# TensorE's next work chosen by the state of banks and engines, products paced by due dates, gelu's 0.5 moved, v kept as two fp16 parts

## The chip, the cores and the metric

One core of a Trainium2 chip runs the whole program. The engines named here are TensorE (PE; its weight loads are PEld), VectorE (DVE), ScalarE (ACT), GpSimd (POOL) and SyncE (SP, which issues the DMAs). The metric is device time in microseconds (us): the median of three runs, lower is better.

## The reference

```python
x = A_x                                               # 1 x 2048 x 512
sa, ca, ga, sb, cb, gb = split(silu(c) @ w_mod, 6)
h = layernorm(x) * (1 + ca) + sa
q, k, v = heads(h @ A_wqkv)                            # 32 heads of 16
x = x + ga * (softmax(q @ k.T * 16 ** -0.5) @ v) @ A_wo
h = layernorm(x) * (1 + cb) + sb
g = shift(gelu(layernorm(h) @ B_w1))                   # quarters moved by +1, -1, +2, -2 rows
x1 = h + g @ B_w2
B = x1 + gelu(layernorm(x1) @ B_w3) @ B_w4             # 1792 hidden columns
out = x + gb * B
```

All of it is in float32, and gelu is the tanh form. Work that feeds TensorE is split into a high and a low part, so that each product of the layers takes three matmuls (high by high, high by low, low by high; the lines of `mm3`).

## The kernel before, in words

The 2048 rows of x are four chunks (`ci`) of 512 queries, the 32 heads are 16 pairs (`pr`), and a chunk with a pair is a unit (`u`): 64 units in all. A unit takes 16 steps, one for each 128 keys; step `s` runs from 0 to 1023. Each step has two rows, one for each head of the pair (`j`), and a row is a pair of matmuls that run side by side on the two halves of the array: a score product `sc` of step `s` (line 1021, keys by queries), and a product `mb` of step `s + LEAD`, 24 steps ahead (line 1005), whose maximum over keys is taken only to know the softmax's shift before the scores come. So there are 2048 rows of `sc` and 2048 of `mb`, and the first 48 rows hold `mb` alone.

What the other engines do with a row: ACT takes the exponential of `sc` into `pt` (line 1017), DVE takes the maximum of `mb` into `mx` (line 1001). The result of the exponential is a 32-bit number whose upper 16 bits serve directly as an fp16 factor; the lower 16 bits are made into a second fp16 factor by `p_low` (line 1072) on POOL, or, when POOL is predicted to be over `LACT` = 800 ns behind ACT, in two halves on ACT (line 127, a helper's). Then TensorE multiplies by v: for each step a pass with the upper factor (line 1098), for each two steps a pass with the lower (line 1095), each pass being four matmuls that run side by side on four column strips of the array. They accumulate in `pv`, one bank for a unit; at its end ACT copies it out (`ac`, line 1116), TensorE transposes it (`ot`, line 1127), DVE sums the parts (`sm`, line 1134) and POOL scales them (line 1138).

PSUM has eight banks: one for `pv` and seven (`NSM`) that rows and all other products share (`Slots`); three rows need six.

All other products (k, q, v of later heads and chunks, the rows of the modulation, and for each finished chunk the tail: A_wo, layer norms, B_w1, B_w2, B_w3, B_w4) are generators in a list of the planner `Sched`. It runs while the kernel is built and writes out one fixed order for each engine; nothing is chosen on the chip. The planner keeps a time for each engine, prices each piece, and hands out the consumers' operations (`chain`, `misc`) to ACT, DVE and POOL when it believes them ready. On the chip each engine follows its list in order, and waits at an instruction until the semaphores are there.

The main loop before goes over fixed blocks of three rows (`GRP`). After each second block come the passes with v that are due (`LAG` blocks behind), and then `fill` adds other products as long as a credit lasts, which grows by a fixed amount for each step (`SC0`, `TAILB`). If the planner thinks that the banks of a block come late, `gap` adds other products ahead of it.

v is kept in DRAM as `Vs`, 192 columns of bf16 for a pair: three bf16 parts, 20 columns apart (`VD`), and an fp16 copy for the pass with the lower factor. `v_tiles` makes it: ACT writes the first part and the fp16 copy, DVE the remainder `vr`, ACT the second part (line 773), POOL the third (line 774).

Gelu's factor 0.5 is multiplied into w2 and w4 when these are prepared (`pieces_gen`, line 899).

Of the kernel before, what the change touches and what calls it, by code (L numbers as in the profile page):

```python
# [8 lines left out]
F32 = mybir.dt.float32  # L9
# [24 lines left out]
VHI = 2.0 ** 39  # L34
VMAX = 2.0 ** 14
VD = 20

SC0 = (32, 900.0, 700.0)
TAILB = (0.0, 500.0, 560.0, 590.0)
# [40 lines left out]
VP = 2  # L80
XB = 4


class Sched:
# [4 lines left out]
    def __init__(self):  # L89
        self.pend = []  # L90
        self.chains = []
        self.gens = []
        self.credit = 0.0
        self.T = {"P": 0.0, "A": 0.0, "D": 0.0, "G": 0.0, "S": 1000.0}
        self.end = 0.0
        self.banks(8)

# [86 lines left out]
    def one(self):  # L184

        self.marks()
        for g in list(self.gens):
# [11 lines left out]
            else:  # L199
                self.credit -= v  # L200
                self.T["P"] += v
# [109 lines left out]
def kernel(ctx, tc, A_x, A_wqkv, A_wo, B_w1, B_w2, B_w3, B_w4, c, w_mod, out):  # L311
# [48 lines left out]
    def v_lo(t):  # L360
        return t[:, :, 128:192].bitcast(F16).rearrange("p a (b n) -> p a b n", b=2)
# [19 lines left out]
    Vs = dr.tile([NP, P, NKT, 192], BF16, name="Vs")  # L381
# [94 lines left out]
    zero = con.tile([4, CH], F32, name="zero")  # L476
# [239 lines left out]
    for i in range(NV):  # L716
        t = qp.tile([P, H // 4, 192], BF16, name=f"vt{i}")
        pool.memset(t, 0.0)
        pool.memset(v_hi(t)[:, :, :, DH:DH + 1], VHI)
        pool.memset(v_lo(t)[:, :, :, 8 + DH:9 + DH], 1.0)  # L720
# [8 lines left out]
    vlive, vrs = [], [0]  # L729
    direct, near = [], set()  # L730

    def v_tiles(w, a, kts):
        wh, wl = halves(w, KT)
        for kt in kts:
            ci, t = divmod(kt, TPC)
            h = hT[ci]
            yield lambda: len(vlive) < NV and vrs[0] < 2 and sch.room() and ("hT", ci) in done
            vrs[0] += 1
# [9 lines left out]
            r = qp.tile([P, H // 4, 2, DH], F32, name="vr", tag="vr", bufs=2)  # L748

            def rest(v=v, b3=b3, r=r, b=b):  # L750
                dve.tensor_tensor(r, b3, v[:, :, :, 0:DH], op=OP.subtract)
                sch.free(b)

            def store(kt=kt, w=w):
                vrs[0] -= 1

# [4 lines left out]
                def gone():  # L761
                    vlive.remove(kt)
                    done.add(("vk", a, kt))
                    if kt % 4 == 3:
# [6 lines left out]
                      ("A", cA(256), lambda vl=vl, b3=b3: act.activation(vl[:, :, :, 8:8 + DH], b3, AF.Copy, scale=1.0 / VHI)),  # L771
                      ("D", cD(256), rest),
                      ("A", cA(256), lambda v=v, r=r: act.activation(v[:, :, :, VD:VD + DH], r, AF.Copy)),
                      ("G", cG(256), lambda v=v, r=r: pool.tensor_tensor(v[:, :, :, 2 * VD:2 * VD + DH], r, v[:, :, :, VD:VD + DH],
                                                                         op=OP.subtract)),
# [97 lines left out]
    def pieces_gen():  # L873
        while True:
# [23 lines left out]
            if nm in ("w2", "w4"):  # L898
                ops.append(("A", cA(), lambda f=f: act.activation(f, f, AF.Copy, scale=0.5)))
# [57 lines left out]
    vst = [at.tile([P, NKT // 4, 192], BF16, name=f"vst{i}") for i in range(4)]  # L957
# [745 lines left out]
```

## Time and profile before

| | us |
|---|---|
| median of three runs | 2002.66 (2001.76 to 2005.11) |
| span of the profiled execution, first to last instruction | 2000.7 |
| start, up to the first score product | 98.2 |
| from the first to the last score product | 1744.5 |
| after the last score product (tail of the last chunk) | 158.0 |
| mean granted TensorE clock | 0.986 of full speed |

The profile has no time of its own for the execution beside the span; the span is 2.0 us under the median. In the rows that follow, a busy time is the union of an engine's instructions. A matmul's end is modelled, and matmuls overlap, so that 96% for PE does not mean that the array is always fed: the distance from one matmul's start to the next one's says more. "Idle before" and the waits name what an engine stood idle for.

### The profile page before, as it was taken

To read this page: it belongs to the slowest core of one execution; us is meant where nothing else is said; L and a number is where in the kernel's file an instruction comes from. 1 tells how busy PE (TensorE), PEld (TensorE's weight loads), DVE (VectorE), ACT (ScalarE), POOL (GpSimd) and SP (SyncE) were. 2 spreads that over 40 slices of the span, in tenths; PEclk is the share of its full clock that TensorE was granted. 3 is DMA by queue.
4 is the path that set the end of the run, shared out by engine and by line. 5 is a ranking of instruction groups with operands and counts; after the bars stand their busy time and mean duration, and the time that the engine had idled before them with its cause. 6 is when DMAs were issued, how large, how long until landed. Compare 5 with 4: busy or idle time off the path is not lost.

```text
span 2000.7 us, 42354 instructions
## 1 busy us (share of the span) xinstructions
PE 1920.9 (96%) x14480; PEld 1146.7 (57%) x14480; DVE 1652.2 (83%) x3010; ACT 1473.6 (74%) x3083; POOL 1676.1 (84%) x1609
## 2 busy tenths in 40 slices
PE   7999999999999999999999999999999999999899
PEld 4655555555455555555455555555555555555798
DVE  7887988888899888888989898898898889883643
ACT  5376888777878777777878787786787878777443
POOL 6287999889999998888999998898899989888532
PEclk8999999999999999999999999999999999999999
DMA  5767677766643334345433333334433343334432
GB/s 184 205 201 228 182 231 218 244 225 192 198 157 111 115 103 143 109 136 162 126 111 92 109 111 114 115 119 148 157 98 100 115 151 107 121 95 147 149 146 90
DMA packets 232352, 293.24 MB, mean 147 GB/s; under 512 B 125876, under 2 KB 177076, under 8 KB 215848
## 3 DMA queue, kind: packets, MB, share of 16 engines
q1 hardware_dynamic: 232136, 290.53, 46.4%
q8 instruction: 115, 1.88, 0.4%
q14 instruction: 101, 0.83, 0.1%
HBM read 225.81 MB, written 62.91 MB: 144 GB/s over the span
## 4 chain that ended last, share of the span: by engine, by line
PE 67%; DVE 16%; ACT 8%; issue 3%; POOL 2%; DMA 2%; SPq 1%; POOLq 0%; ACTq 0%; DVEq 0%
PE mb L1005 14%; PE sc L1021 10%; PE pv L1098 10%; DVE mx L1001 9%; PE w L339 7%; PE w L343 6%; PE w L341 6%; PE pv L1095 4%; ACT pt L1017 4%; POOL pt L1072 2%; DVE xs L1421 1%; DVE sq L1418 1%; DMA vst<-Vs 1%; PE mr L644 1%; PE ot L1127 1%
## 5 line engine op out<-in xcount | busy, mean ns | idle before, releaser
L1072 POOL TENSOR_SCALAR pt<-pt 128x1024 f16<-128x1024 uint16 x988 | 1312.5, 1365 | 132.6 <-ACT pt L1017 125.4
L1001 DVE TENSOR_REDUCE mx<-mb 128x1 f32<-128x512 f32 x2048 | 1281.0, 683 | 76.0 <-PE mb L1005 54.5
L1017 ACT ACTIVATE pt<-sc 128x512 int32<-128x512 f32 x2048 | 1090.8, 606 | 272.3 <-PE mb L1005 164.9
L1005 PE MATMUL mb<-kst,qtl 64*128 64x512 f32 x2048 | 752.1, 454 | 49.0 <-ACT pt L1017 16.1
L1021 PE MATMUL sc<-qtl,kst 64*128 64x512 f32 x2048 | 716.4, 444 | 2.6 <-DVE A L329 0.6
L1005 PEld LDWEIGHTS mb<-kst,qtl 64*128 64x128 f32 x2048 | 348.7, 193 | 254.5 <-DVE mx L1001 91.4
L1021 PEld LDWEIGHTS sc<-qtl,kst 64*128 64x128 f32 x2048 | 335.6, 186 | 153.5 <-DVE mx L1001 47.1
L1098 PE MATMUL pv<-pt,vst 128*32 128x512 f16 x4096 | 358.2, 397 | 0.1
L1095 PE MATMUL pv<-pt,vst 128*17 128x512 f16 (+1 forms) x2048 | 213.7, 394 | 2.2 <-POOL pt L1072 1.7
L1098 PEld LDWEIGHTS <-vst 128*32 128x32 bf16 x4096 | 90.9, 95 | 167.6 <-issue 108.8
L339 PE MATMUL w<-A,wr 128*128 128x256 f32 (+2 forms) x576 | 175.3, 304 | 0.3 <-ACT A L333 0.3
L1428 POOL TENSOR_TENSOR g<-xs,g 128x256 fp32r<-128x256 f32 (+2 forms) x144 | 103.2, 718 | 83.4 <-ACT g L1427 81.3
L341 PE MATMUL w<-A,wr 128*128 128x256 f32 (+2 forms) x576 | 169.8, 295 | 0.5 <-DVE A L329 0.3
L343 PE MATMUL w<-A,wr 128*128 128x256 f32 (+2 forms) x576 | 167.7, 291 | 0.0
L339 PEld LDWEIGHTS w<-A,wr 128*128 128x128 f32 x576 | 109.6, 190 | 35.4 <-DVE mx L1001 10.3
L339 PE MATMUL w<-wr,g 128*128 128x512 f32 x288 | 119.2, 414 | 0.6 <-ACT g L1427 0.6
L341 PEld LDWEIGHTS w<-A,wr 128*128 128x128 f32 x576 | 109.9, 191 | 12.4 <-issue 11.3
L343 PE MATMUL w<-wr,g 128*128 128x512 f32 x288 | 114.7, 398 | 0.2 <-POOL g L1428 0.2
L341 PE MATMUL w<-wr,g 128*128 128x512 f32 x288 | 113.6, 394 | 0.0
L343 PEld LDWEIGHTS w<-A,wr 128*128 128x128 f32 x576 | 109.8, 191 | 6.7 <-issue 6.7
L1535 DVE TENSOR_TENSOR x<-x,w 128x512 f32<-128x512 f32 x64 | 43.9, 687 | 82.0 <-PE w L343 82.0
L1424 ACT ACTIVATE sq<-w 128x256 f32<-128x256 f32 (+2 forms) x144 | 55.7, 387 | 68.8 <-PE w L343 66.0
(151 smaller groups left out, 2103.8 us busy)
## 6 DMA issues: line engine op xcount, KB each, us to landing
wr<-Ws SPq DMA_DIRECT2D x80, 1024.0 KB
kst<-Ks SPq DMA_DIRECT2D x189, 256.0 KB
vst<-Vs SPq DMA_DIRECT2D x252, 192.0 KB
qtl<-Qs SPq DMA_DIRECT2D x192, 64.0 KB
Vs<-vt SPq DMA_DIRECT2D x32, 384.0 KB
Ws<-wq SPq DMA_DIRECT2D x40, 256.0 KB
Ws<-wst SPq DMA_DIRECT2D x40, 256.0 KB
wst<-in_B_w_dram SPq DMA_DIRECT2D x36, 256.0 KB
```

The lines of the kernel that those rows point to most:

```text
L339: te.matmul(o, lh, rh, start=first, stop=False)
L341: te.matmul(o, lh, rl, start=False, stop=False)
L343: te.matmul(o, ll, rh, start=False, stop=last)
L1001: end = sch.crit("D", 605, e + PX, lambda: dve.reduce_max(mxs[u][:, j, g, c:c + 1], b, axis=AX.X))
L1005: return ready, lambda: te.matmul(b, lhs, kst[u % 3][r, c * CH:(c + 1) * CH], start=True, stop=True), after
L1017: ea = sch.crit("A", 480, e + PX, lambda: act.activation(pt[s][:, j], b, AF.Exp))
L1021: return ready, lambda: te.matmul(b, kst[u % 3][r, kt * P:(kt + 1) * P], qst[u][r], start=True, stop=True), after
L1072: e_low[s] = XP["G"] + sch.crit("G", 1345, ready, lambda: pool.tensor_scalar(o, i, 0.5, 1.0, op0=OP.mult, op1=OP.mult))
L1095: te.matmul(acc[r:r + n, :], v[:, (kt + i) % 4, c - n:c].bitcast(F16), pt[s + i].bitcast(F16)[:, j, 0::2], start=False, stop=kt == NKT - 2 ...
L1098: te.matmul(acc[r:r + 32, :], v[:, kt % 4, r:r + 32], pt[s].bitcast(F16)[:, j, 1::2], start=kt == 0, stop=False, skip_group_check=True)
L1424: sch.chain(("A", cA(n), lambda: act.activation(sq, b, AF.Square)), ("D", cD(n), cube), ("A", cA(n), lambda: act.activation(sq, sq, AF.Tan ...
L1428: ("G", cG(n), lambda: pool.tensor_tensor(lo, xs, hi, op=OP.subtract)), (None, 0, end), bank=b)
```

## The change

The main loop is new. It goes row by row and keeps a mode of TensorE (`r` rows, `c` passes with v, `o` other products), with 95 ns for a change of mode and 107 ns more for going into rows. Inside a burst of up to three rows the next row is taken if its banks are at most 300 ns away. Otherwise the loop looks whether passes with v are ready (up to six, taken at once if there are four, or if fewer fit into the time until banks are free), then adds other products until the banks are expected. The credit that allows other products grows with each row by what is left to the next due date (`DUES`: step, and the us of products to have been issued by then). `p_low` of a step is handed out at least one step later than before. The wait for a unit's k and q may come up to four steps later, and one wait at each chunk (`oT`) becomes a condition of a generator.

v is kept as two fp16 parts, 32 columns apart, in the place of three bf16 ones; the scale moves into powers of two. Step 773 on ACT and step 774 on POOL are gone, `vr` is gone, and DVE writes the second part itself. The pass with the lower factor uses 17 columns for every strip, where it was 17 and 25. `sm` sums two parts.

The 0.5 of gelu is no longer multiplied into w2 and w4 (line 899 gone); the layer norms ahead of both gelus are halved instead, by a second operation in an instruction that was there, and gelu's own constants are doubled.

```diff
-VHI = 2.0 ** 39
-VMAX = 2.0 ** 14
-VD = 20
-SC0 = (32, 900.0, 700.0)
-TAILB = (0.0, 500.0, 560.0, 590.0)
+VHI = 2.0 ** 15
+VMAX = 1.0
+VLO = 2.0 ** -20
+PLO = 2.0 ** -20
+VD = 32
+DUES = ((20, 67.7), (60, 87.3), (85, 95.9), (122, 115.8), (150, 130.7), (205, 149.7), (245, 167.7),
+        (505, 270.0), (765, 395.7), (1012, 527.8))
+BTOP, BLOW = 1200.0, 300.0
+SWITCH, ENTER = 95.0, 107.0
+EARLY, STAY, BACK, GRACE = 300.0, 300.0, 150.0, 0.0
+OWE, CTOP = 500.0, 5000.0
+CHIGH, CMIN, CMOST, PTLOW, PLAG = 2500.0, 4, 6, 2, 1
...
             def rest(v=v, b3=b3, r=r, b=b):
-                dve.tensor_tensor(r, b3, v[:, :, :, 0:DH], op=OP.subtract)
+                dve.tensor_tensor(v[:, :, :, VD:VD + DH], b3, v[:, :, :, 0:DH], op=OP.subtract)
...
-                      ("A", cA(256), lambda v=v, r=r: act.activation(v[:, :, :, VD:VD + DH], r, AF.Copy)),
-                      ("G", cG(256), lambda v=v, r=r: pool.tensor_tensor(v[:, :, :, 2 * VD:2 * VD + DH], r, v[:, :, :, VD:VD + DH],
-                                                                         op=OP.subtract)),
...
-            if nm in ("w2", "w4"):
-                ops.append(("A", cA(), lambda f=f: act.activation(f, f, AF.Copy, scale=0.5)))
...
-                dve.tensor_scalar(mv[:, 1:2], mv[:, 1:2], EPS, None, op0=OP.add)
+                dve.tensor_scalar(mv[:, 1:2], mv[:, 1:2], EPS, 4.0 if half else 1.0, op0=OP.add, op1=OP.mult)
...
+    x, end, seen, burst = -2 * LEAD, 2 * NS, -99, 0
+    while x < end or pvs or acs:
...
+        nc_ = cols()
+        if can:
+            if sch.mode == "r" and burst < GRP:
+                slack = one - now
+                row = slack <= STAY
+            else:
...
+                slack = max(st, dry - CROW - PX - EARLY) - enter - now
+                row = slack <= BACK and (sch.mode == "r" or sch.credit < CHIGH and not (nc_ >= CMIN and len(pts) <= PTLOW))
+        if not row:
+            n = 0
+            if nc_ >= CMIN or nc_ and slack >= nc_ * CCOL + (sch.mode != "c") * SWITCH:
+                do_cols(nc_)
+                n = nc_
+            else:
+                stop = now + max(slack, 0.0) + GRACE
+                while (sch.T["P"] < stop or sch.credit > CHIGH) and sch.credit > (-OVER if sch.open else 0.0) and sch.one():
+                    n += 1
...
+        if row:
+            do_row(x, max(now, one - enter))
```

How the order moves is seen on TensorE at a product of B_w4 (`w`, line 339 and the two after it; `wr` the weights, `g` the activations) in the third chunk's attention. Before, a burst of three rows, and then the first three of the product's twelve matmuls; the other nine follow without a break:

```order
L1005 MATMUL mb<-kst_153,qtl_151 128x512
L1021 MATMUL sc<-qtl_605,kst_607 128x512 x2
L1005 MATMUL mb<-kst_153,qtl_151 128x512 x2
L1021 MATMUL sc<-qtl_605,kst_607 128x512
L339 MATMUL w_20852<-wr,g_20100 128x512
L341 MATMUL w_20852<-wr,g_20100 128x512
L343 MATMUL w_20852<-wr,g_20100 128x512
```

Now the same kind of product is in three pieces of six, four and two matmuls, with rows and passes with v between; this is the second piece and the three rows behind it:

```order
L357 MATMUL w_20135<-wr,g_19461 128x512
L359 MATMUL w_20135<-wr,g_19461 128x512
L361 MATMUL w_20135<-wr,g_19461 128x512
L357 MATMUL w_20135<-wr,g_19461 128x512
L1015 MATMUL mb<-kst_600,qtl_598 128x512
L1031 MATMUL sc<-qtl_151,kst_153 128x512 x2
L1015 MATMUL mb<-kst_600,qtl_598 128x512 x2
L1031 MATMUL sc<-qtl_151,kst_153 128x512
```

What moved: twelve matmuls in one stretch have become three stretches, and there are more changes between rows, passes and products.

On DVE, the additions of four such products into `x` (line 1535, now 1549), with the maxima `mx` of the rows between them. Before:

```order
L1001 TENSOR_REDUCE mx<-mb 128x1 x10
L1535 TENSOR_TENSOR x_7924<-x_7924,w_20600 128x512
L1001 TENSOR_REDUCE mx<-mb 128x1 x6
L1051 TENSOR_REDUCE mf<-mx 128x8
L1134 TENSOR_REDUCE sm<-ot 128x136
L1001 TENSOR_REDUCE mx<-mb 128x1 x3
L1144 RECIPROCAL rc<-sm 128x8
L1001 TENSOR_REDUCE mx<-mb 128x1 x3
L1535 TENSOR_TENSOR x_14262<-x_14262,w_20709 128x512
L1001 TENSOR_REDUCE mx<-mb 128x1 x6
L1535 TENSOR_TENSOR x_14264<-x_14264,w_20852 128x512
L1001 TENSOR_REDUCE mx<-mb 128x1 x5
```

Now:

```order
L1549 TENSOR_TENSOR x_7683<-x_7683,w_19776 128x512
L1011 TENSOR_REDUCE mx<-mb 128x1 x3
L1148 TENSOR_REDUCE sm<-ot 128x136
L1158 RECIPROCAL rc<-sm 128x8
L1011 TENSOR_REDUCE mx<-mb 128x1 x9
L1549 TENSOR_TENSOR x_13530<-x_13530,w_19996 128x512
L1011 TENSOR_REDUCE mx<-mb 128x1 x9
L1549 TENSOR_TENSOR x_13532<-x_13532,w_20135 128x512
```

What moved: six maxima stood between two additions before, and nine stand there now in the rows shown, since a product is spread over more rows.

On ACT at the start, where the tiles of v (`vt`) are made: two operations on the product `v` and one on `vr` for each tile before,

```order
L770 ACTIVATE vt_166<-v 128x8x2x16
L771 ACTIVATE vt_166<-v 128x8x2x16
L773 ACTIVATE vt_166<-vr 128x8x2x16
L770 ACTIVATE vt_170<-v 128x8x2x16
L771 ACTIVATE vt_170<-v 128x8x2x16
L773 ACTIVATE vt_170<-vr 128x8x2x16
```

and two for each tile now:

```order
L784 ACTIVATE vt_166<-v 128x8x2x16
L785 ACTIVATE vt_166<-v 128x8x2x16
L784 ACTIVATE vt_170<-v 128x8x2x16
L785 ACTIVATE vt_170<-v 128x8x2x16
L784 ACTIVATE vt_174<-v 128x8x2x16
```

What moved: the third operation of each tile is gone, and the next tile's stands in its place; on POOL the operation behind it (line 774) is gone too.

More of the change, by code (lines that the diff above doesn't have):

```diff
@@ L474 @@
     kst, qtl = [], []
-    zero = con.tile([4, CH], F32, name="zero")
+    zero = con.tile([4, P], F32, name="zero")
     pool.memset(zero, 0.0)
@@ L956 @@
     qst, mxs, osb = {}, {}, {}
-    vst = [at.tile([P, NKT // 4, 192], BF16, name=f"vst{i}") for i in range(4)]
+    vst = [at.tile([P, NKT // 4, 192], F16, name=f"vst{i}") for i in range(4)]
     direct += vst
@@ new lines, in col_at, with cols @@
+    def col_at(y):
+        s, lo = y
+        if lo:
+            return max(e_low[s], e_low[s + 1]) if s in e_low and s + 1 in e_low else LATE
+        return max(e_hi[s], v_free[0] if s % NKT == 0 else 0.0) if s in e_hi else LATE
+    def cols():
+        n, t = 0, sch.T["P"] + (sch.mode != "c") * SWITCH
+        for y in pvs[:CMOST]:
+            if n and y[0] % NKT == 0 and not y[1]:
+                break
+            if col_at(y) > t + 20:
+                break
+            t += CCOL
+            n += 1
+        return n
@@ L1605 @@
+    sch.mode = "o"
+    while x < end or pvs or acs:
         if acs:
             ac_copy()
[L1607 to L1616 removed]
@@ L1632 @@
-        sch.gap(start)
-        sch.flush(need)
-        sch.T["P"] = max(sch.T["P"], start) + CIN
-        low = sorted(e_exp)
-        for s, i in row:
-            for fn in row_pair(s, i):
-                fn()
+        can = x < end
+        if can:
+            s, i = divmod(x, 2)
+            if x == LENDS:
+                sch.most = MOST
+            if i == 0 and seen != s:
+                seen = s
+                before(s)
+                if s >= 0 and s % 16 == 0:
+                    drain(("shift", s // 16))
+            can = i or s < 0 or bool(pts)
@@ L1639 @@
+        now, row, slack = sch.T["P"], False, LATE
+        if can:
+            need = (s >= 0) + (s + LEAD < NS)
+            sch.flush(need)
+            free = sorted(sm.t)
+            one = free[need - 1 + 2 * (s < 0)]
+            if one >= LATE:
+                one = free[need - 1]
+            enter = (sch.mode != "r") * (SWITCH + ENTER)
+        else:
+            for q in sorted(e_exp):
+                p_low(q)
             while second:
                 second.pop(0)()
-        while second:
-            second.pop(0)()
@@ new lines @@
+        if not row:
[3 more added lines that the diff above has]
+                n = nc_
+            else:
+                stop = now + max(slack, 0.0) + GRACE
+                while (sch.T["P"] < stop or sch.credit > CHIGH) and sch.credit > (-OVER if sch.open else 0.0) and sch.one():
+                    n += 1
+            if not n:
+                if not can or one - enter > now + 100.0:
+                    sch.T["P"] = now + 50.0
+                else:
+                    row = True
```

173 lines of the change are left out of this document (86 added, 87 removed).

## The prediction

> **What bounds the kernel now.** I read the page first, then the busy times by stretch, then the waits of each engine, and last the order of matmuls in time.
>
> ```profile
> span 2000.7 us, 42354 instructions
> PE 1920.9 (96%) x14480; PEld 1146.7 (57%) x14480; DVE 1652.2 (83%) x3010; ACT 1473.6 (74%) x3083; POOL 1676.1 (84%) x1609
> ...
> PE 67%; DVE 16%; ACT 8%; issue 3%; POOL 2%; DMA 2%; SPq 1%; POOLq 0%; ACTq 0%; DVEq 0%
> ```
>
> The first row of engines gives no winner: four are between 74% and 96%. The shares in the last row are of the chain that ended last, and two thirds of it run through TensorE. The stretches show where the time lies (columns: start and end, length, busy time of PE, PEld, DVE, ACT, POOL with counts, clock, DMA share, GB/s): the start up to the first score, four quarters of attention, and the last chunk's tail.
>
> ```profile
> 0.00:98.20 98.20, 80.81 (x389) 56.96 (x389) 78.74 (x145) 43.38 (x84) 46.65 (x64) 0.93 0.62 193
> 98.20:553.30 455.10, 434.98 (x3267) 242.58 (x3267) 380.72 (x647) 360.62 (x744) 403.29 (x343) 0.98 0.69 212
> 553.30:983.20 429.90, 416.17 (x3322) 234.63 (x3318) 377.55 (x699) 333.12 (x708) 383.44 (x371) 0.99 0.42 131
> 983.20:1411.90 428.70, 418.54 (x3338) 240.19 (x3334) 379.89 (x698) 336.37 (x703) 389.44 (x369) 1.00 0.37 113
> 1411.90:1842.70 430.80, 422.46 (x3350) 244.21 (x3349) 358.81 (x664) 338.86 (x711) 390.32 (x377) 1.00 0.39 122
> 1842.70:2000.70 158.00, 147.90 (x826) 128.09 (x825) 76.49 (x159) 61.25 (x136) 62.99 (x89) 0.98 0.36 130
> ```
>
> Start and tail hold nothing that the change moves much, so attention, 1744.5 us, is the question. Its sum:
>
> ```profile
> sum 1744.50, PE 1692.16 PEld 961.62 DVE 1496.97 ACT 1368.98 POOL 1566.50; mean PE 423.04 PEld 240.40 DVE 374.24 ACT 342.24 POOL 391.62
> ```
>
> Idle there: POOL 178, DVE 248, ACT 375. PE's 1692 is no measure, so I price it by starts:
>
> ```profile
> 1062.68 0.41 PE L1095 MATMUL pv<-pt,vst 128*17 128x512 f16 x4
> 1062.91 0.41 PE L1098 MATMUL pv<-pt,vst 128*32 128x512 f16 x4
> 1063.25 0.39 PE L339 MATMUL w<-A,wr 128*128 128x256 f32 x1
> 1063.47 0.28 PE L341 MATMUL w<-A,wr 128*128 128x256 f32 x1
> 1063.59 0.28 PE L343 MATMUL w<-A,wr 128*128 128x256 f32 x1
> 1063.71 0.28 PE L339 MATMUL w<-A,wr 128*128 128x256 f32 x1
> 1063.92 0.50 PE L1021 MATMUL sc<-qtl,kst 64*128 64x512 f32 x1
> ...
> 1066.05 0.50 PE L1005 MATMUL mb<-kst,qtl 64*128 64x512 f32 x1
> 1066.38 0.39 PE L1005 MATMUL mb<-kst,qtl 64*128 64x512 f32 x1
> 1066.62 0.39 PE L1005 MATMUL mb<-kst,qtl 64*128 64x512 f32 x1
> 1066.94 0.41 PE L1098 MATMUL pv<-pt,vst 128*32 128x512 f16 x4
> ```
>
> Each pass of 512 columns follows the last after 0.23 us (1062.68, 1062.91), each 256-column product after 0.12 (1063.47, 1063.59, 1063.71). Every change of kind costs about 0.1 us more: pass to product 0.34 for 0.23, product to row 0.21 for 0.12, row to pass 0.32 for 0.23. The first step inside products (0.22 for 0.12) and inside rows (0.33 for 0.24) costs another 0.1. So a stretch costs, beyond its work, 0.21 us for rows, 0.20 for products and 0.11 for passes.
>
> With the order's counts between the first and last score, PE needs: rows 465 us, passes 352, other products 468 (512 columns at 0.23, 256 at 0.12, 128 at 0.11, a transpose at 0.105), together 1285; and 620 stretches of rows, 351 of passes and 362 of products at those prices, 241. That is 1526 of 1744.5, or 87.5%; the other 218 us PE waits. For what, the weight loads say:
>
> ```profile
> PEld mb L1005 <- DVE mx L1001: 89.3, 216, 3.8
> PEld mb L1005 <- ACT pt L1017: 82.0, 197, 1.4
> PEld sc L1021 <- DVE mx L1001: 47.1, 114, 1.0
> PEld sc L1021 <- ACT pt L1017: 36.6, 98, 0.6
> ```
>
> 255 us in 625 waits, for banks that DVE and ACT have not emptied (some of it is the entry into rows). One such wait, between two bursts with nothing put between:
>
> ```profile
> 1038.83 0.51 PE L1005 MATMUL mb<-kst,qtl 64*128 64x512 f32 x1
> 1039.74 0.51 PE L1005 MATMUL mb<-kst,qtl 64*128 64x512 f32 x1 [0.41 <-DVE mx L1001]
> ```
>
> 0.91 us from row to row, where 0.23 is the work. On the other side the consumers wait for PE and for each other:
>
> ```profile
> DVE mx L1001 <- PE mb L1005: 52.0, 102, 2.0
> DVE x L1535 <- PE w L343: 49.3, 37, 2.0
> ...
> POOL pt L1072 <- ACT pt L1017: 125.2, 133, 4.9
> ```
>
> DVE stands 52.0 us at a maximum whose row isn't there, and 49.3 at the addition of a product that PE, in a stretch of twelve matmuls, has not ended; POOL stands 125.2 for exponentials. No engine is full: the kernel is bound by the hand-over between PE, DVE/ACT and POOL through seven banks, with PE's list as the thread.
>
> **The change, part by part.** Durations for the other engines:
>
> ```profile
> L1072 POOL TENSOR_SCALAR pt<-pt 128x1024 f16<-128x1024 uint16 x988 | 1312.5, 1365 | 132.6 <-ACT pt L1017 125.4 <-ACT mf L1052 1.7 <-POOL pt L1072 1.1
> ...
> L127 ACT ACTIVATE pt<-pt 128x512 f16<-128x512 uint16 x72 | 57.8, 808 | 0.0
> ...
> L1134 DVE TENSOR_REDUCE sm<-ot 128x136 f32<-128x408 f32 x64 | 36.8, 575 | 5.4 <-PE ot L1127 5.4
> ...
> L774 POOL TENSOR_TENSOR vt<-vr,vt 128x256 bf16<-128x256 f32 x32 | 22.6, 708 | 35.3 <-ACT vt L773 25.9 <-DMA qtl<-nm 5.3 <-DMA Vs<-vt 3.5
> ...
> L773 ACT ACTIVATE vt<-vr 128x256 bf16<-128x256 f32 x32 | 13.8, 432 | 6.4 <-DVE vr L751 6.4
> ...
> L899 ACT ACTIVATE wst<-wst 128x512 f32<-128x512 f32 x18 | 11.7, 650 | 0.0
> ```
>
> *v in two parts.* POOL loses 32 x 0.708 = 22.6 us, ACT 13.8. The reduction `sm` reads 272 columns a partition where it read 408: 64 x 0.575 = 36.8 us, at most a third less, 12. DVE's remainder stays one instruction per tile. TensorE's passes keep their number and their 512 columns. Each tile's chain is two operations shorter.
>
> *Gelu.* 18 x 0.650 = 11.7 us of ACT go; ACT idles 375 us, so the path gets nothing. The halving rides in an instruction that was there. The zero rows keep their 61 DMAs, in smaller pieces. Both count zero: the 375 us of ACT's idle time cover the one, and of the other no wait of PE is among its longest; if these rows came late, a unit's first rows would wait. The waits written into the loop (for a unit's k and q, for `ac`) are the planner's: they bend the order, and no queue on the chip gets a new one, so they are priced with the order.
>
> *Lower factors.* In the order POOL has 963 of them (988 before) and ACT 122 halves (72): POOL loses 25 x 1.365 = 34.1 us, ACT gains 50 x 0.808 = 40.4. Attention then asks 1566.5 - 22.6 - 34.1 = 1510 of POOL, 1369 + 40.4 - 13.8 - 11.7 = 1384 of ACT, some 1488 of DVE.
>
> *TensorE.* The work is the same but for 6 us of products that now lie after the first score (290 other matmuls ahead of it, 320 before): 1291. The stretches become 700, 637 and 569: 147 + 70 + 114 = 331 us, 90 more. PE's need rises from 1526 to 1622. This is the change's price, and on the path wherever PE wasn't waiting; its return is that waits are filled. Of 82 bursts of five rows or more without anything between, 19 are left.
>
> The Trainium skill's page TensorEngine Tiling (Array Packing), Key Properties, says that changing the tiling mode, not only the tile, drains TensorE. The 0.1 us per change above agrees with it; it gives no figure, and by that rule alone more changes mean a longer time, which is the first rival's result.
>
> *Banks held longer.* Of about 335 products in attention 209 are now spread over several bursts (124 before), and each holds one of seven banks meanwhile. No row prices this. From below: nothing, where the bank would have stood empty. From above: one row wait more for each of the 85, at 89.3 / 216 = 0.41 us, is 35 us. I take nothing, as the loop fills such waits, and keep 35 for the range.
>
> *The sum.* 1622 us must be turned into time by the share of it that PE can keep up. Before it was 0.875 on average, 0.92 over the last quarter (a need of 396 in 430.8), and best in these two stretches of four units:
>
> ```profile
> 1203.70:1307.70 104.00, 103.14 (x831) 59.50 (x833) 90.64 (x163) 77.68 (x164) 90.08 (x79) 1.00 0.35 107
> 1638.50:1743.10 104.60, 103.81 (x850) 61.01 (x850) 91.81 (x166) 79.66 (x170) 90.44 (x80) 1.00 0.41 129
> ```
>
> By the same prices PE's need there was 99.5 of 104.0 and 100.2 of 104.6: 0.957. I take 0.955, nearest to these, because the new loop puts work into waits everywhere, and because POOL and DVE allow it: 1622 / 0.955 = 1698 us, in which POOL is busy 89% (90% before) and DVE 88% (86%). Attention loses 46 us. Start and tail stay: 98.2 + 1698 + 158.0 = 1954. The median of the runs stands 2.0 over the profiled span, so 1956. What is late next is POOL and DVE, both near 90%.
>
> **Rivals.** *Slower: the changes of kind cost more than the waits they fill.* The share stays at the last quarter's 0.92, where PE was pressed longest: 1622 / 0.92 = 1763, plus start and tail and 2 us: 2021; with the 35 us of banks, 2056. It decides below 1622 / 1744.5 = 0.93. For it: the chain is 67% PE, and the due dates load the units behind each chunk's start, where by the order PE's need is 107 to 113 us for four units (88 to 98 before, units 16 to 19, 32 to 35, 48 to 51). Against: each change is put where a wait was expected.
>
> *Much faster: PE's waits vanish.* At 0.985, 1647 us of attention, total 1907. POOL would be busy 92% and DVE 90%. For it: POOL's 57 us less, and shorter stretches without rows, so that DVE is fed more evenly. Against: no quarter had POOL over 91% (390.32 of 430.80).
>
> *No change: the loop turns waits into changes of kind, one for one.* 90 us of 218 become overhead, 122 stay: 2002. For it: a two-matmul piece of 0.24 us costs 0.20 to start and leave.
>
> **How the numbers follow.** Forecast, 1930 to 1990: 0.45. Much faster, under 1930: 0.18. A small gain, 1990 to 1998: 0.04. Within 0.2%, which is about what a measurement of this kernel can tell from no change: 0.08. Slower: 0.25. So faster 0.67, same 0.08, slower 0.25. The range runs from 1905, just under the much faster case, to 2025, just over the slower one without the banks; I leave 0.06 below and 0.11 above it.
>
> **What would show it.** Right: PE's waits for `mx` and `pt` at rows fall from 255 us to under 150, DVE's wait at the `x` additions falls under 25 of 49.3, attention near 1700, start and tail within 4 us of 98.2 and 158.0. Each change of kind still costs 0.1. Wrong: row waits that stay near 200, then the time is at or above 2002; units 16 to 19, 32 to 35 and 48 to 51 would show it first. If row waits are gone and the time is still over 1990, the prices of the changes were too low. A DMA wait at a unit's first row would be a cause that I count at nothing.

## The result, and the profile after

The changed kernel is slower: 2060.39 us (median of four, 2059.79 to 2061.07) against 2002.21, a ratio of 1.030 (95% interval 1.028 to 1.032). The forecast was 1956, in a range of 1905 to 2025. The page and the stretches of after, in the columns shown for before (start, four quarters of attention, tail):

```profile
span 2059.3 us, 42254 instructions
...
PE 1982.6 (96%) x14480; PEld 1138.1 (55%) x14480; DVE 1669.8 (81%) x3010; ACT 1489.2 (72%) x3083; POOL 1681.7 (82%) x1552
...
PE 68%; POOL 11%; DVE 9%; ACT 6%; issue 2%; DMA 2%; SPq 1%; POOLq 0%; ACTq 0%; DVEq 0%
```

```profile
0.00:96.40 96.40, 77.16 (x357) 53.86 (x357) 78.07 (x143) 37.98 (x70) 38.27 (x53) 0.91 0.59 186
96.40:567.30 470.90, 453.90 (x3306) 245.17 (x3305) 380.58 (x650) 356.25 (x724) 394.77 (x315) 0.98 0.67 207
567.30:1004.00 436.70, 427.86 (x3320) 231.55 (x3316) 382.14 (x700) 341.75 (x721) 390.44 (x364) 1.00 0.41 129
1004.00:1454.80 450.80, 440.85 (x3372) 240.91 (x3368) 390.55 (x705) 345.02 (x717) 399.56 (x370) 1.00 0.37 116
1454.80:1897.50 442.70, 433.61 (x3316) 237.61 (x3312) 362.86 (x659) 344.97 (x717) 393.78 (x364) 0.99 0.36 113
1897.50:2059.30 161.80, 149.25 (x824) 129.04 (x824) 75.62 (x159) 63.27 (x140) 64.86 (x90) 0.97 0.32 119
```

The loss lies in attention: 1801.1 us for 1744.5. Start (96.4) and tail (161.8) stayed within 4 us. In the chain that ended last POOL has gone from 2% to 11%, the first sign that the forecast had left something out on that engine.

The waits in attention, those of the weight loads at rows, of DVE, ACT and POOL (engine, what it waited for, total, times, longest):

```profile
PEld mb L1015 <- DVE mx L1011: 59.8, 161, 1.7
...
PEld mb L1015 <- ACT pt L1027: 40.5, 112, 1.3
...
PEld sc L1031 <- DVE mx L1011: 29.0, 79, 1.6
PEld sc L1031 <- ACT pt L1027: 25.6, 83, 1.1
```

```profile
DVE mx L1011 <- PE mb L1015: 137.6, 267, 3.9
DVE mx L1011 <- PE sc L1031: 42.9, 80, 3.5
...
DVE x L1549 <- PE w L361: 1.0, 2, 0.7
```

```profile
ACT pt L1027 <- PE mb L1015: 242.9, 298, 4.6
ACT pt L1027 <- PE sc L1031: 80.0, 99, 5.5
```

The same waits before, as far as the prediction doesn't show them:

```profile
DVE mx L1001 <- PE sc L1021: 15.4, 32, 1.6
```

```profile
ACT pt L1017 <- PE mb L1005: 164.9, 213, 2.5
ACT pt L1017 <- PE sc L1021: 84.8, 68, 3.7
```

TensorE waits for banks 154.9 us where it waited 255, and the additions of `x` hardly wait (1.0 for 49.3): what the new loop was forecast to do, it does. But DVE now stands 180.5 us at maxima whose row isn't there (67.4 before), and ACT 322.9 at exponentials (249.7 before). The rows come late, though they wait less for banks than before.

On POOL, a run of lower factors before, and one after (start, length from first start to last end, count):

```profile
1107.81 3.94 POOL L1072 TENSOR_SCALAR pt<-pt 128x1024 f16<-128x1024 uint16 x3
```

```profile
1121.14 4.24 POOL L1082 TENSOR_SCALAR pt<-pt 128x1024 f16<-128x1024 uint16 x3
```

One instruction takes 1.36 us in both. Three in a row take 3.94 before, (3.94 - 1.36) / 2 = 1.29 us from start to start, and 4.24 now, 1.44 us. Over the whole trace the median from start to start, of neighbours less than 1.9 us apart, is 1293 and 1438 ns. Before, the next one started while the records still showed the last as running; now it starts 0.08 us after its end. The sum of POOL's gaps under 100 ns in attention went from 7.9 to 92.7 us.

### The profile page after: what moved, and what is told of

Read it like the earlier page. It is cut to its first block, busy times and chain, and to the rows that moved or that the text cites. A ratio compares the mean times of both kernels' runs of the same rounds, so it can differ in the third digit from the quotient of the medians.

```text
span 2059.3 us, 42254 instructions
## 1 busy us (share of the span) xinstructions
PE 1982.6 (96%) x14480; PEld 1138.1 (55%) x14480; DVE 1669.8 (81%) x3010; ACT 1489.2 (72%) x3083; POOL 1681.7 (82%) x1552
## 4 chain that ended last, share of the span: by engine, by line
PE 68%; POOL 11%; DVE 9%; ACT 6%; issue 2%; DMA 2%; SPq 1%; POOLq 0%; ACTq 0%; DVEq 0%
PE mb L1015 13%; PE sc L1031 10%; PE pv L1108 9%; PE w L357 7%; PE w L359 7%; POOL pt L1082 7%; PE w L361 7%; PE pv L1105 6%; DVE mx L1011 5%; ACT pt L1027 3%; PE ot L1140 1%; DMA vst<-Vs 1%; SPq L121 1%; ACT pt L142 1%; PE q L357 1%
## 5 line engine op out<-in xcount | busy, mean ns | idle before, releaser
L1011 DVE TENSOR_REDUCE mx<-mb 128x1 f32<-128x512 f32 x2048 | 1296.3, 683 | 186.2 <-PE mb L1015 139.2
L1015 PE MATMUL mb<-kst,qtl 64*128 64x512 f32 x2048 | 731.2, 447 | 22.3 <-ACT pt L1027 5.9
L1031 PE MATMUL sc<-qtl,kst 64*128 64x512 f32 x2048 | 707.8, 441 | 4.4 <-DVE mx L1011 1.6
L1108 PE MATMUL pv<-pt,vst 128*32 128x512 f16 x4096 | 367.7, 393 | 5.1 <-DMA vst<-Vs 4.4
L1105 PE MATMUL pv<-pt,vst 128*17 128x512 f16 x2048 | 233.2, 396 | 15.4 <-POOL pt L1082 14.7
L1108 PEld LDWEIGHTS <-vst 128*32 128x32 f16 x4096 | 113.3, 94 | 124.6 <-issue 72.2
L1105 PEld LDWEIGHTS <-vst 128*17 128x17 f16 x2048 | 59.2, 88 | 174.4 <-issue 163.4
L357 PE MATMUL w<-wr,g 128*128 128x512 f32 x288 | 121.2, 421 | 0.9 <-ACT g L1441 0.6
L361 PE MATMUL w<-wr,g 128*128 128x512 f32 x288 | 119.3, 414 | 0.2 <-POOL g L1442 0.2
L359 PE MATMUL w<-wr,g 128*128 128x512 f32 x288 | 118.8, 412 | 0.0
L142 ACT ACTIVATE pt<-pt 128x512 f16<-128x512 uint16 x122 | 98.9, 819 | 0.0
```

Source lines behind the costliest of these rows:

```text
L142: fn()
L357: te.matmul(o, lh, rh, start=first, stop=False)
L359: te.matmul(o, lh, rl, start=False, stop=False)
L361: te.matmul(o, ll, rh, start=False, stop=last)
L1011: end = sch.crit("D", 605, e + PX, lambda: dve.reduce_max(mxs[u][:, j, g, c:c + 1], b, axis=AX.X))
L1015: return ready, lambda: te.matmul(b, lhs, kst[u % 3][r, c * CH:(c + 1) * CH], start=True, stop=True), after
```

## The experiments

In the table, "need" is TensorE's by the prediction's prices, counted in each run's own trace; "wait" is attention less need; the last column is the median from start to start of POOL's lower factors. "Old" and "new" are the main loop; "v" stands for the arithmetic of v and gelu. Each ratio is to runs of before that were made beside the run's own, with medians from 1994.87 to 2002.21 us; the stretches of before are of one profile, so a difference of a few us between the stretches of two kernels says little. In e1, e7, e10 and e11 the lower factors come out too large and in e2 too small, so the output of these five isn't the reference's; it changes no instruction but its number.

| kernel | loop, v, factor | ratio to before (95%) | attention, tail | need, wait | POOL ns |
|---|---|---|---|---|---|
| before | old, old, 0.5 | 1 | 1744.5, 158.0 | 1534, 210 | 1293 |
| after | new, new, 2^-20 | 1.030 (1.028 to 1.032) | 1801.1, 161.8 | 1630, 171 | 1438 |
| e1 | new, new, 0.5 | 1.016 (1.013 to 1.019) | 1773.9, 159.0 | 1630, 144 | 1293 |
| e2 | old, old, 2^-20 | 1.030 (1.027 to 1.033) | 1798.1, 158.9 | 1534, 264 | 1435 |
| e3 | old, new, 2^-20 | 1.037 (1.034 to 1.040) | 1803.9, 170.1 | 1524, 279 | 1436 |
| e4 | new, old, 0.5 | 1.012 (1.009 to 1.015) | 1766.9, 160.1 | 1627, 140 | 1293 |
| e7 | e1, products whole | 1.020 (1.018 to 1.022) | 1769.4, 161.2 | 1563, 206 | 1292 |
| e10 | e1, long bursts | 1.104 (1.101 to 1.106) | 1947.3, 161.2 | 1504, 444 | 1286 |
| e11 | old, new, 0.5 | 1.009 (1.007 to 1.011) | 1741.8, 169.6 | 1524, 217 | 1291 |
| e12 | old, new, 0.5 x 2^-19 | 1.000 (0.999 to 1.001) | 1741.0, 158.8 | 1536, 205 | 1293 |
| e13 | new, new, 0.5 x 2^-19 | 1.012 (1.010 to 1.014) | 1764.1, 159.3 | 1634, 130 | 1293 |
| e18 | e13, even pace | 1.004 (1.002 to 1.005) | 1741.1, 168.9 | 1628, 113 | 1293 |

### Which part: the factor, the loop, the arithmetic

The change alters the number in `p_low` too: 0.5 became `PLO`, 2^-20. e1 takes that back in the changed kernel, and e2 puts it into the kernel before, on POOL and in ACT's halves:

```diff
-PLO = 2.0 ** -20
+PLO = 0.5
```

> The changed kernel with one number other: the factor by which the lower parts of the exponentials are multiplied is 0.5, as before the change, and not 2^-20 (the order of every engine stays that of the changed kernel; the lower factors, and with them the output, come out too large, which changes no instruction). Theory F (factor): in the changed kernel each of these POOL instructions starts 0.08 us after its neighbour's end, where before it started 0.03 to 0.09 ahead of it; the small factor does this, costs POOL about 0.15 us each, 963 times, some 140 us, and POOL holds the rest up. Then the start-to-start of two of them falls from 1.44 to 1.29 us and the time falls by 40 us or more, to 1960 to 2020. Theory L (loop): the 90 us of added changes of kind on TensorE are what made it slower, and POOL only shows it. Then the time stays within 10 us of 2060, whatever POOL's spacing.

```diff
-                o, i, 0.5, 1.0, op0=OP.mult, op1=OP.mult))
+                o, i, 2.0 ** -20, 1.0, op0=OP.mult, op1=OP.mult))
```

> The kernel before with one number other: the factor for the lower parts is 2^-20 in the place of 0.5, on POOL and in the halves on ACT (the order stays that of before; the lower factors come out too small, so the output lacks most of them). Theory F: POOL's spacing goes from 1.29 to 1.44 us; 988 times 0.15 is 148 us on an engine that is busy 1566 of 1745 us of attention, so the time rises by 40 to 90 us, to 2040 to 2090. Theory L: the time stays at 2002 within 5 us, as the order is the same.

Attention in e2, in the columns of the stretches:

```profile
97.70:1895.80 1798.10, 1712.49 (x13269) 967.52 (x13268) 1495.64 (x2707) 1371.66 (x2865) 1627.56 (x1457) 0.98 0.45 141
```

The counts are those of before (x13269, x2707, x2865, x1457), the length is 53.6 us more: the number alone, in an unchanged order, costs about what the whole change does. POOL is busy 1627.6 us and stands in short gaps for 107, together 96% of attention; of its 170 us in longer gaps 64 are left. In the new loop the same number costs 28 us (after against e1). POOL had more room there: 237 us in longer gaps, 130 with the slow number. That this room is why it costs less is argued, not shown.

e3 is the old loop with the new arithmetic, e4 the new loop with the old arithmetic:

```diff
-VHI = 2.0 ** 39
-VMAX = 2.0 ** 14
-VD = 20
+VHI = 2.0 ** 15
+VMAX = 1.0
+VLO = 2.0 ** -20
+PLO = 2.0 ** -20
+VD = 32
...
-                dve.tensor_tensor(r, b3, v[:, :, :, 0:DH], op=OP.subtract)
+                dve.tensor_tensor(v[:, :, :, VD:VD + DH], b3, v[:, :, :, 0:DH], op=OP.subtract)
```

> The old main loop and planner with the new arithmetic alone: v as two fp16 parts, gelu's 0.5 moved, the factor 2^-20. Theory F: POOL has 32 instructions fewer but 0.15 us more on each lower factor, so slower than before: 2030 to 2080. Theory L: the arithmetic only takes work away, so 1985 to 2002.

> The new main loop, due dates and waits with the old arithmetic: v as three bf16 parts, the 0.5 of gelu on w2 and w4, the factor 0.5. Theory F: the loop is not what costs, so 1960 to 2010. Theory L: as slow as the whole change or slower, since POOL and ACT also keep the work that the new arithmetic drops: 2055 to 2080.

The new loop alone, with the fast number, costs 1.2%; it isn't the arithmetic. e11 is e3 with `PLO = 0.5`:

> The old loop and the new arithmetic, with the factor 0.5 (lower factors too large); with 2^-20 it took 2075 us. Theory F (the factor is 58 us here as in the kernel before, and the rest of the new arithmetic helps nothing in the old loop): 2008 to 2022. The other way: without the factor the arithmetic is worth its removed work, some 20 us of POOL, 1980 to 2000.

Attention is then 1741.8, 3 us under before, so in the old loop too the slow number is worth some 60 us of e3. Of the 0.9% that is left, some 18 us, 12 lie in the tail (169.6 us for 158.0), since the old pace leaves 822 matmuls of tail products after the last score, 755 before; the rest is not placed. e12 keeps the values of 2^-20 and writes them as 0.5 x 2^-19, gives products 5% more room in the last chunk, and lets the planner count an fp16 transfer as two bytes an element (the first two are shown, against e3):

```diff
-                o, i, PLO, 1.0, op0=OP.mult, op1=OP.mult))
+                o, i, 0.5, PLO * 2.0, op0=OP.mult, op1=OP.mult))
...
-TAILB = (0.0, 500.0, 560.0, 590.0)
+TAILB = (0.0, 500.0, 560.0, 620.0)
```

> Old loop, new arithmetic of v and gelu, lower factor written as 0.5 times 2^-19 (the same values as 2^-20); the last budget of products 620 ns for each step (590 before), so that 818 matmuls follow the last score, as before (902 in the run with 590). Theory (POOL's slow start-to-start time belongs to the number 2^-20 in the instruction; the arithmetic itself is worth nearly nothing; the 12 us of longer tail came from the old pace): spacing on POOL 1.29 us, attention 1740 to 1755, tail 158, median 1998 to 2010, within 0.5% of the kernel before. Rival (the small lower factors cost time elsewhere, on TensorE's passes or at reading): attention over 1790.

Ratio 1.0002 (0.999 to 1.0013): with the tail at its old length (158.8 us), v in two parts and gelu's 0.5 are worth nothing, which is what the prediction's sum gave them. e13 is the changed kernel with the same pair and the same count of bytes:

> The changed kernel with the lower factor written as 0.5 times 2^-19: same values as 2^-20, and the planner counts an fp16 transfer as two bytes an element. Theory: spacing on POOL falls from 1.44 to 1.29 us and the median from 2060 to about 2032 (as with the factor 0.5), still 1.5% over the kernel before, since the new loop by itself costs that. Rival (the whole loss is the slow factor): within 0.5% of the kernel before.

Its 2020.44 us are the loop's own loss, 1.2%, with the values as the change wants them.

### What in the number is slow

The new lower factor could have been slow for its results: those of lower parts under 64 (of 65536) come out under 2^-14 and are subnormal in fp16. e5 scales by 2^-14 in place of 2^-20 (`VLO` by 2^-26, so that the products keep their size), e8 does so in the old loop, and e6 adds 64 first:

> The changed kernel with the same product of scales shared out otherwise: the lower factors times 2^-14 (2^-20 in the change), v's copy for that pass times 2^-26 (2^-20). The smallest nonzero lower factor is then 2^-14, the smallest normal fp16 number, where with 2^-20 every value under 64 of 65536 comes out subnormal. The factor 0.5 with the same order took 2032 us, 2^-20 took 2060. Theory S (subnormal results slow POOL): spacing 1.29 us and 2025 to 2037 us. Theory C (the small factor itself does it, whatever comes out): spacing 1.44 us and 2055 to 2065.

> The changed kernel, but POOL adds 64 to the lower part before the product with 2^-20 (two operations of one instruction, as now; the lower factors come out too large by 64 in up to 65535, and the halves made on ACT are left as they are). No result on POOL is subnormal, the factor is the changed kernel's. Theory S: spacing 1.29 us, 2025 to 2037 us. Theory C: spacing 1.44, 2055 to 2065.

> The old loop with the new arithmetic and the scales 2^-14 and 2^-26. With 2^-20 this took 2075 us. Theory S: POOL's spacing is 1.29 us again, POOL and ACT have less to do than before, 1985 to 2003 us. Theory C: 2070 to 2080. If the spacing is 1.29 and the time is still 15 us or more over 2002, then the new arithmetic bends the old planner's order to the worse.

All three stay slow: 1.032, 1.033 and 1.038, at 1437 to 1439 ns; and e12 and e13, which have the results of 2^-20, are fast. So it isn't the results' size. Three maps of the kernel before then give each unit, modulo 8, a pair of numbers of its own (the edit that all three share is shown); their lower factors aren't those of the kernel before, and of these runs only the profile is read.

```diff
-                o, i, 0.5, 1.0, op0=OP.mult, op1=OP.mult))
+                o, i, *KINDS[s // NKT % 8], op0=OP.mult, op1=OP.mult))
```

> The kernel before, with another pair of factors on POOL's lower factors for each unit of eight (the rest of the output follows from them and is off): 0.5 x 1; 0.25 x 1; 2^-4 x 1; 2^-8 x 1; 2^-20 x 2^19; 0.5 x 2^-19; 2 x 0.25; 0.375 x 1. Two results so far: subnormal results are not what slows POOL, since 2^-14 and 64 added first were as slow as 2^-20 (1.44 us from start to start, 1.29 with 0.5). Theory V (the size of the results): 2^-20 x 2^19, 2 x 0.25, 0.25 and 0.375 run at 1.29, 0.5 x 2^-19 at 1.44, and 2^-4 or 2^-8 marks the place. Theory I (the number written in the instruction): 2^-20 x 2^19 runs at 1.44 too. If every pair but 0.5 x 1 runs at 1.44, it is that one pair that is special.

> The kernel before with a pair of factors for each unit modulo 8: (2^-3, 1), (2^-5, 1), (2^-6, 1), (2^-7, 1), (2^-12, 1), (2^-16, 1), (2^-19, 1), (1, 2^-20); the lower factors' values are not those of the kernel before. Theory (a property of the first number): (1, 2^-20) takes 1.29 us from start to start; of the others some take 1.44 and some 1.29, with nothing between. Rival (size of the result or of the second number): (1, 2^-20) takes 1.44, and the rest are ordered by size.

> The kernel before with a pair of factors for each unit modulo 8: (2^-9, 1), (2^-10, 1), (2^-13, 1), (2^-15, 1), (2^-22, 1), (4, 2^-8), (1.5 times 2^-20, 1), (2^-11, 2^-5); the lower factors' values are not those of the kernel before. Theory from the two maps so far (for 2^-k it is k modulo 8 that decides: 4, 5 and 6 are slow, the others fast, in either of the two numbers): 2^-9, 2^-10, 2^-15 take 1.29 us from start to start; 2^-13, 2^-22 and 4 (k = -2) take 1.44; 1.5 times 2^-20 takes 1.44 if only the exponent counts; 2^-11 with 2^-5 takes 1.44 because of the second. Rival (chance in the numbers tried): three or more of the eight come out otherwise.

The medians from start to start fall on two values, with nothing between:

| | numbers |
|---|---|
| 1283 to 1296 ns | 2, 0.5, 0.375, 2^-2, 2^-3, 2^-7, 2^-8, 2^-9, 2^-10, 2^-15, 2^-16, 2^-19 (each with a fast second number); 0.5 with 2^-19 |
| 1432 to 1439 ns | 4 with 2^-8, 2^-4, 2^-5, 2^-6, 2^-12, 2^-13, 2^-20, 1.5 x 2^-20, 2^-22; 1 with 2^-20; 2^-11 with 2^-5; 2^-20 with 2^19 |

For 2^-k it is the remainder of k by 8 that decides: 4, 5 and 6 are slow, in either of the two numbers. The first two maps suggested it, the third was forecast by it and came out in all eight pairs. The rows of the third, units 26 to 28 (2^-13, 2^-15, 2^-22) after the end of unit 25 (2^-10):

```profile
835.54 6.53 POOL L1073 TENSOR_SCALAR pt<-pt 128x1024 f16<-128x1024 uint16 x5
...
846.74 7.09 POOL L1073 TENSOR_SCALAR pt<-pt 128x1024 f16<-128x1024 uint16 x5
...
861.26 7.08 POOL L1073 TENSOR_SCALAR pt<-pt 128x1024 f16<-128x1024 uint16 x5
...
880.52 6.50 POOL L1073 TENSOR_SCALAR pt<-pt 128x1024 f16<-128x1024 uint16 x5
...
903.20 7.14 POOL L1073 TENSOR_SCALAR pt<-pt 128x1024 f16<-128x1024 uint16 x5
```

Five in a row take 6.53, then 7.09, 7.08, then 6.50, then 7.14: the same instruction on the same shapes, and four steps of 1.29 or 1.43 us. Why a number's exponent should do that stays open.

### Why the new loop loses by itself

e7 takes changes of kind away: a product that is open is finished before rows come again. e10 lets bursts go on to six rows and wait up to 700 ns for a bank inside.

```diff
-                while (sch.T["P"] < stop or sch.credit > CHIGH) and sch.credit > (-OVER if sch.open else 0.0) and sch.one():
+                while (sch.T["P"] < stop or sch.credit > CHIGH or sch.open) and sch.credit > (-4000.0 if sch.open else 0.0) and sch.one():
```

> The changed kernel with the factor 0.5 (2032 us), and its loop changed in one place: once a product has begun, its matmuls are added until it is complete, so that no product is spread over bursts (lower factors too large, as with 0.5). By the order the stretches of products in attention fall from 569 to 303, and by the prices of the prediction PE's need from 1622 to 1556 us; no bank is held over a burst. Theory P (TensorE's changes of kind and banks held by split products are what the loop costs): attention falls by 25 to 65 us, to 1710 to 1750, and the time to 1967 to 2007. Theory D (short stretches are what keeps DVE and ACT fed; long ones starve them): row waits and DVE's idle time at product additions rise, and the time is 2025 or more.

```diff
-EARLY, STAY, BACK, GRACE = 300.0, 300.0, 150.0, 0.0
+EARLY, STAY, BACK, GRACE = 300.0, 700.0, 150.0, 0.0
...
-            if sch.mode == "r" and burst < GRP:
+            if sch.mode == "r" and burst < 2 * GRP:
```

> The changed kernel with the factor 0.5 (2032 us; lower factors too large) and two numbers of its loop: a burst may have six rows for three, and the next row of a burst is waited for up to 700 ns for 300. By the order there are 411 bursts of rows in attention for 700, and 363 stretches of products for 569, so PE's need falls from 1622 to 1496 us. The run with whole products has shown that PE's need alone is not it: 66 us less need, the same time. Theory B (each burst costs DVE a turn-around: before, DVE idles 246 us in 621 bursts, with the new loop 258 in 701, with whole products 270 in 685, 0.37 to 0.40 us each): DVE's idle time falls to some 160 us and the time by 60 to 100, to 1930 to 1970. Theory D (a row that waits for its own banks inside a burst holds PE's passes and products up, and these then come late): PE waits 200 us or more, and the time is 2010 or more.

Against e1, e7's need falls by 67 us and its waits rise by 62, so that attention gains 4.5 us of the 67 (and the start is 6 us longer). The waits are those that the new loop had removed: rows wait 231 us for banks (159 in e1), and the additions of `x` wait again (0.5 us in e1):

```profile
PEld mb L1015 <- ACT pt L1027: 91.1, 247, 1.2
PEld mb L1015 <- DVE mx L1011: 69.9, 170, 1.7
```

```profile
DVE x L1549 <- PE w L361: 54.6, 42, 2.0
```

e10's need falls by 126 and its waits rise by 300, of which 240 are at rows for banks (399 for 159). Its longest:

```profile
PEld mb L1015 <- DVE mx L1011: 216.6, 437, 1.1
```

So to take changes of kind away, in these two manners, does not make the loop faster: what need loses, waits win. The Trainium skill's page TensorEngine Tiling (Array Packing), Key Properties, says that changing the tiling mode drains TensorE; the 0.1 us at each change agrees with it. By itself it doesn't give the time here: e7 has 67 us less of it and 4.5 us less attention.

e14 no longer holds a burst back until DVE or ACT is within 300 ns of running dry, and e17 hands lower factors out at once and not a step later, both on e13:

```diff
-EARLY, STAY, BACK, GRACE = 300.0, 300.0, 150.0, 0.0
+EARLY, STAY, BACK, GRACE = 3000.0, 300.0, 150.0, 0.0
```

> The same as the run of the changed loop with 0.5 times 2^-19, but the loop no longer holds rows back until the consumers' queues run down to 300 ns (EARLY 3000): a burst may begin when its banks are free. Theory A (the new loop loses because it starts rows late, so that DVE and ACT stand idle for them): DVE's idle time for rows falls from about 162 us to under 110, and the median from 2032 to under 2015. Theory B (stretches of changes and waits trade one for one, whatever the rule of choice): stretches 699, 635 and 559, need 9 us less, median 2025 to 2040.

```diff
-CHIGH, CMIN, CMOST, PTLOW, PLAG = 2500.0, 4, 6, 2, 1
+CHIGH, CMIN, CMOST, PTLOW, PLAG = 2500.0, 4, 6, 2, 0
```

> The changed loop with 0.5 times 2^-19, and lower factors handed out as soon as they may be, not at least one step later (PLAG 0). Theory A (the delay of a step leaves POOL idle and TensorE without passes, and is part of the loop's loss): POOL's idle time falls from 223 us to under 190 and the median to under 2010. Theory B (need and waits trade one for one): stretches 725, 697 and 589, need 11 us more, median 2015 to 2030.

Neither moves it: 1.0116 (1.0101 to 1.0132) and 1.0094 (1.0068 to 1.0121) against e13's 1.0117 (1.0097 to 1.0136), attention 1764.4 and 1763.4 against 1764.1. The place was then looked for in time. Here are the last two units of the second chunk and the first two of the third, before and in e13:

```profile
936.20:983.20 47.00, 45.03 (x369) 23.01 (x368) 43.65 (x78) 37.97 (x80) 42.16 (x41) 1.00 0.51 161
983.20:1035.50 52.30, 50.68 (x387) 27.10 (x384) 47.92 (x89) 40.48 (x79) 47.56 (x50) 1.00 0.26 70
```

```profile
936.40:978.20 41.80, 41.21 (x332) 19.46 (x329) 40.37 (x72) 38.04 (x78) 39.04 (x34) 1.00 0.31 87
978.20:1041.90 63.70, 61.40 (x446) 33.36 (x442) 56.36 (x110) 52.88 (x104) 54.80 (x66) 1.00 0.29 92
```

In e13 products have run out before the chunk ends (332 matmuls for 369), and the credit grows to its cap meanwhile (5000 at steps 512 and 768 in the planner's own count, under 500 again at 544 and 800). When the next products are there, the credit is over `CHIGH`, and the loop issues them whether or not a bank is awaited: 446 matmuls for 387, in 63.7 us for 52.3. The engines behind TensorE are full in those last units: DVE is busy 40.37 of 41.80 us and POOL 39.04, so these units get hardly shorter with fewer products. A stretch of 6 us at the chunk's start, of e13:

```profile
996.00:1002.00 6.00, 6.00 (x45) 3.24 (x44) 4.23 (x7) 3.15 (x6) 3.31 (x3) 1.00 0.24 66
```

PE is never idle, while DVE has 4.23 us of work, ACT 3.15 and POOL 3.31, behind eleven matmuls of 512 columns without a row (from 994.17 to 996.9). One such run is not the difference: before has three of eleven or twelve such matmuls in this place (at 1007.45, 1013.22 and 1029.73). What is new is how many products fall on it. The starts of the three later chunks (53.6, 52.3 and 56.8 us before) take 64.4, 63.7 and 64.8 in e13: 30 us together, of which the ends of the chunks ahead of them (149.8 before, 136.7) give 13 back. e18 makes the pace even; due dates, floor and cap of the credit change together:

```diff
-DUES = ((20, 67.7), (60, 87.3), (85, 95.9), (122, 115.8), (150, 130.7), (205, 149.7), (245, 167.7),
-        (505, 270.0), (765, 395.7), (1012, 527.8))
-BTOP, BLOW = 1200.0, 300.0
+DUES = ((20, 67.7), (60, 87.3), (85, 95.9), (122, 115.8), (150, 130.7), (205, 149.7), (245, 167.7), (508, 271.0), (764, 396.0), (1018, 521.0))
+BTOP, BLOW = 1200.0, 0.0
...
-OWE, CTOP = 500.0, 5000.0
+OWE, CTOP = 500.0, 1500.0
...
-        return min(BTOP, max([BLOW] + [(1000.0 * w - sch.spent) / (d - s) for d, w in DUES if d > s]))
+        return min(BTOP, max([BLOW] + [(1000.0 * w - sch.spent) / (d - s) for d, w in DUES if d > s][:1]))
```

> The changed loop with 0.5 times 2^-19 and an even pace of products: the credit grows only toward the next due date, the due dates of the chunks are 508, 764 and 1018 with the work that exists, and the credit is capped at 1500 (5000 before), so that products are never forced in long stretches at a chunk's start. In the run without this, products end one or two units before each chunk's end (41 to 50 us for the last two units) and the first two units of the next chunk take 64 to 65 us. Theory A (this uneven pace is the loop's loss): the first two units of the chunks take under 58 us, attention falls from 1764 to under 1735, and with 51 more products in the tail (801 for 750, some 7 us) the median is under 2000. Theory B (waits and changes trade one for one however the products are spread): attention stays within 15 us of 1764, less the 7 us of work that has gone into the tail; median 2010 to 2025.

```profile
920.80:971.30 50.50, 49.98 (x404) 27.03 (x402) 45.35 (x82) 38.47 (x83) 44.50 (x40) 1.00 0.46 148
971.30:1026.20 54.90, 53.79 (x396) 27.25 (x394) 50.20 (x92) 43.59 (x86) 48.30 (x54) 1.00 0.34 107
```

The three starts are now 53.7, 54.9 and 50.2 us. With the ends ahead of them the three places take 313.6 us, 329.7 in e13 and 312.5 before; at the one shown the sum is the same (105.4 for 105.5), with 800 matmuls in it for 778. Attention is 1741.1, the median 2005.05, 1.004 of before. Both theories missed by a little: A had said attention under 1735 and a median under 2000, B that attention stays within 15 us of 1764 less 7. Some 7 us of the 23 are the work that went into the tail (168.9). So the uneven pace was the larger part of the loop's loss, 0.8% of 1.2%, some 16 us of 23, as much as the three places give back; with it gone, the loop's attention is about that of before (1741.1 for 1744.5) with 94 us more need and 97 us less wait. None of these kernels is faster than the kernel before; e12 equals it.

## Why the prediction was wrong

**The number and the price of the changes were right.** The need was forecast at 1622 us, and the prices give 1630 for the trace of after. The steps themselves are the same before and after (medians from start to start): 0.32 us from a product of 512 columns to a row, 0.33 from a pass to a product, 0.34 and 0.33 from a row to a pass. Row waits were to fall from 255 to under 150 (154.9), the `x` additions' wait under 25 (1.0), start and tail to stay within 4 us: all nearly so, and the time rose nevertheless. For row waits gone and a time over 1990 the prediction blamed prices that are too low; these steps show that they aren't.

**The step "Lower factors" failed.** It counted 25 instructions less at 1.365 us and costed the new number in the others at nothing, without a word. The number made the 963 instructions 0.145 us longer from start to start, some 140 us of POOL (busy time and short gaps in attention: 1671 us in after, 1537 in e1), and that isn't in their duration, which stayed 1.36. POOL was to be 89% busy; with its short gaps it stood at (1578.6 + 92.7) / 1801.1 = 93%. In this order it cost 28 us of the 58 (after against e1).

**The step "The sum" failed: the share of 0.955.** Attention took 103 us more than the forecast's 1698; 27 of these are the slow number, and 76 the share: the same order without the slow number has 1630 / 1773.9 = 0.919 (e1). It is 1634 / 1764.1 = 0.926 in e13, and 1628 / 1741.1 = 0.935 with an even pace. 0.955 came from the two best stretches of before, units 40 to 43 and 56 to 59, which lie in the middle of a chunk. It was also read a little high: counted in the trace by the same prices they need 97.5 us of 104.0 and 99.1 of 104.6, not 99.5 and 100.2, which is 0.94 and gives 1725 us of attention, still a gain. There the new loop has it too: by the same prices 0.95 to 0.98 in the second and third four units of every chunk of e13. But the first four of the three later chunks have about 0.9, and the last four of each chunk 0.84 to 0.93. The best parts were taken for the whole.

**The "slower" rival had the place, and the size of the loop's own loss, not the cause.** Its share of 0.92 gives 1763 us of attention; e13 has 1764.1, which is partly luck, since need and share were both a little higher (1634 and 0.926). The 2060 of the changed kernel lies beyond its 2021. Units 16 to 19, 32 to 35 and 48 to 51 did show it first: 110.1, 107.8 and 111.8 us before, 119.8, 122.3 and 124.5 after. But it put the loss on changes of kind, and e7 has 67 us of these less for 4.5 us of attention. The larger part of the loop's loss sat in the pace of products, whose due dates it had named as a reason beside.

**The "no change" rival had the mechanism** of what is left: with the fast number and an even pace need and wait trade one for one. It said 90 us; e18 has 94 for 97. Its time, 2002, is about that of e18 (1.004 of before); the changed kernel has the slow number and the uneven pace besides.

**What was right at nothing:** v in two parts, gelu and the zero rows (e12). The 35 us for banks held longer stayed unmeasured by itself; e7, where no product holds a bank over a burst, gains 4.5 us of attention in all. A slip that nothing rests on: the much faster rival's parts add up to 1905, not 1907.

Of the loss of 58 us, then, 28 are the number. Of the other 30, some 16 are the uneven pace (e13 to e18), 7 are what e18 still loses, with a tail 11 us longer, and the rest lies between e1 and e13, whose orders differ a little; it is not taken apart.

## What to carry to other kernels

A constant in an instruction is a part of its cost: when a change rewrites one, time the instruction from start to start before and after, since the duration in the records doesn't show it. Fill an engine's waits only as far as the work in hand lasts: a credit that grows while there is nothing to issue comes back as too many products in one place, where they lengthen the time, after too few in another, where the other engines were full and little time was saved. And a share of busy time taken from the best stretch of a trace holds for that stretch; look at the worst place of the new order first, which the order's count of products named here beforehand.

## What the runs showed of the hardware

POOL's multiplication of 128x1024 uint16 into fp16 follows itself after 1.29 us or after 1.44, by the number it multiplies by: for 2^-k slow where k modulo 8 is 4, 5 or 6, for the 24 pairs tried, in either of the two numbers. The size of the result doesn't matter in the runs that tried it: the same results come fast from 0.5 x 2^-19 and slow from 2^-20. The record of one instruction is 1.36 us long in both cases. The cause is not known, and other operations (but for e6's addition ahead of the product) and shapes weren't tried.
